# Linear attention into a gated MLP: one load on another queue, a longer row of opening matmuls, and another order of the first tile's second product

## The chip, the cores and the metric

The kernel runs on one core of one Trainium2 chip. A time is the time of one execution on the device, in microseconds (us). Eight runs of the kernel before gave a median of 286.97 us, from 286.65 to 289.56.

## The reference

Attention without a softmax feeds a two-layer MLP with a gate. `q`, `k` and `v` are 8 batches x 8 heads x 576 rows x 64, in float32.

```python
kv  = np.einsum('bhsd,bhse->bhde', k, v)
out = np.einsum('bhsd,bhde->bhse', q, kv)
rms = np.sqrt(np.mean(out * out, axis=-1, keepdims=True) + 1e-06)
x   = (out / rms * g_norm), its heads side by side: 4608 x 512
h   = x @ w_in                       # 512 x 2048
g   = h * (1.0 / (1.0 + np.exp(-1.702 * h)))
y   = g @ w_out                      # 2048 x 512
```

## The kernel before

**Tiles.** The 4608 rows are cut into nine row tiles of 512: one for the first 512 rows of each batch, `t` = 0 to 7, and a last one, `t` = 8, for the eight remainders of 64 rows. For each tile `dense` computes the hidden layer (`Hidden.mm`, L438: 16 column blocks of 128, four matmuls each; `gate` on ScalarE, L447) and then the product with `w_out` (`project`, L475: four row blocks `mo` of 128, sixteen matmuls `fo` each). While tile `t` is in `dense`, the attention of batch `t + 1` is woven into it. `units1` and `units2` hold that work: a unit filed under a number runs after the hidden block, or the step of the product, with that number. A step is one matmul of L475. So the numbers in `at2(...)` set where on TensorE a piece of attention stands, and also the order in which its instructions reach VectorE and ScalarE.

**Order.** The program runs with a schedule written out by hand: each engine takes its instructions in the order in which the Python code emits them, and semaphores do the rest.

**The opening.** Nothing can be woven into batch 0, so it runs by itself, head pair by head pair (four pairs): transpose `q` (L393), `kv` (L376), a copy to `kvb` (L383), `out` (L259), the sum of squares `ss` (L339), `ln` and `rs` on ScalarE (L341, L347), and `apply` on VectorE (L353), which writes the MLP's input `xT`. Before that TensorE runs 64 short matmuls on zeros (L572) and some long ones (`busy`, L562) whose results nobody reads.

**Queues.** SP's queue loads pair 0 of `k`, `q` and `v` of batch 0 in float32 (L147); VectorE and ScalarE cast them to half precision (L553 to L555). All else in the opening comes through GpSimd's queue, which casts as it loads: pairs 1 to 3 of batch 0 (`early_load`, L91), `w_in` (L166), `w_out` (L193), and `q`, `k`, `v` of batch 1 (L91, L112). Eight semaphores serve that queue in turn, so that the ninth load waits for the landing of the first, the tenth for that of the second, and so on. GpSimd also sets two constants, `ident` and `ones2` (L152 to L163), ahead of its first load.

**Batch 1 inside tile 0.** This is where the `at2` numbers of the diff belong. `pack_k` (L218) copies a pair of `k` into `kpad` on VectorE, `kv` (L227) multiplies it with `v`, `keep_kv` (L240) copies the result of two pairs to `kvb` on VectorE, `out` (L259) uses that, and `ss` and `apply` follow as above. PSUM has eight banks: three with the tag "att", three with "hT" and two with "o". In tile 0 the row blocks `mo` 0 and 1 of the second product hold two of the "hT" banks and `ss` has the third; the hidden blocks of tile 1 need all three again.

The steps of tile 0 are ordered by hand ("deep"), since `w_out` is still landing:

```python
steps = [(mo, 4 * i + k) for i in range(3) for mo in range(4) for k in range(4)]
steps += [(mo, f + k) for f in (12, 14) for mo in range(2) for k in range(2)]
steps += [(mo, 12 + k) for mo in (2, 3) for k in range(4)]
```

Of the kernel before, what the change touches and what calls it, by code (L numbers as in the profile page):

```python
# [12 lines left out]
P = 128  # L13
# [3 lines left out]
def kernel(  # L17
# [10 lines left out]
    nc = tc.nc  # L28
# [4 lines left out]
    NPAIR = H // 2  # L33
    FO = DFF // P
    KO = DM // P
# [8 lines left out]
    PE_ = 96  # L44
# [29 lines left out]
    vbuf = const.tile([P, NPAIR, 2 * NJ * D], F16)  # L74
# [5 lines left out]
    w_in_sb = const.tile([P, KO, DFF], F16)  # L80
# [6 lines left out]
    def early_src(n, b, c0, c1):  # L87
        return srcs[n][b, 2 * c0 : 2 * c1].rearrange("h (p j) d -> p h (j d)", j=NJ)

    def early_load(n, b, c0, c1):  # L90
        nc.gpsimd.dma_start(  # L91
            out=raw[n][0:PE_, c0:c1, :].rearrange("p c (l x) -> p (c l) x", l=2),
            in_=early_src(n, b, c0, c1),
        )
# [45 lines left out]


    first = {}
    for n in "kqv":
        first[n] = stage.tile([P, H, J * D], F32, name=f"{n}f", tag=f"{n}f")
        first[n] = first[n].rearrange("p h x -> p (h x)")[0:PE_, 0 : 2 * NJ * D]
        dst, src = first[n].rearrange("p (h x) -> p h x", h=2), early_src(n, 0, 0, 1)
        nc.sync.dma_start(out=dst, in_=src)  # L147
    g_row = const.tile([1, D], F32)
    nc.scalar.dma_start(out=g_row, in_=g_norm.unsqueeze(0))
    nc.vector.memset(ident, 0.0)  # L150
    nc.vector.memset(kvb[1], 0.0)
    nc.gpsimd.affine_select(  # L152
        out=ident,
        in_=ident,
# [6 lines left out]
    nc.gpsimd.memset(ones2, 0.0)  # L161
    nc.gpsimd.memset(ones2[0:D, 0:D], 1.0)
    nc.gpsimd.memset(ones2[D:P, D:P], 1.0)  # L163

    def load_w_in(f0, f1, k0=0, k1=KO):
        nc.gpsimd.dma_start(  # L166
            out=w_in_sb[:, k0:k1, f0 * P : f1 * P],
            in_=moe_w_in[k0 * P : k1 * P, f0 * P : f1 * P].rearrange(
                "(ko ki) f -> ki ko f", ki=P
            ),  # L170
        )

    for c in range(1, NPAIR):
        for n in "qkv":
            early_load(n, 0, c, c + 1)
            if c == NPAIR - 1 and n == "q":
                load_w_in(0, 4, 0, 1)
    load_w_in(0, 4, 1, 2)
    load_w_in(0, 4, 2, KO)
    load_w_in(4, GROUP)  # L180
    load_w_in(GROUP, 8)
# [267 lines left out]
    def dense(t, units1, units2, group, deep, hid=None):  # L449
        hid = hid or Hidden(t)  # L450
        gT = hid.gT
        if group and t:
            order = [(ko, fo) for part in ((0, 3, 1, 2), range(4, group)) for ko in (0, 1) for fo in part]
            order += [(ko, fo) for ko in range(2, KO) for fo in range(group)]
            for ko, fo in order:
                pool = (ps_h, "hT") if fo < 3 else (ps_a, "att") if fo == 3 else (ps_o, "o")
                hid.mm(ko, fo, *pool)
            for fo in range(group):
                hid.gate(fo)
        for fo in range(FO):  # L460
            if fo >= group:
                for ko in range(KO):
                    hid.mm(ko, fo)
                hid.gate(fo)
            for u in units1.get(fo, ()):
                u()

        osb = osbs[t] = opool.tile([P, 4, DM], F32, name="osb", tag="osb")
        os = {}

        def project(mo, fo):
            if fo == 0:
                pool, tag = (ps_h, "hT") if deep and mo < 2 else (ps_o, "o")
                os[mo] = pool.tile([P, DM], F32, name="o", tag=tag)
            nc.tensor.matmul(  # L475
                os[mo],
                gT[:, fo, mo * P : (mo + 1) * P],
                w_out_sb[:, fo, :],
                start=(fo == 0),
                stop=(fo == FO - 1),  # L480
            )
            if fo == FO - 1:
                by_act = mo % 2 if deep or t == B else 0 < t < B - 1 and mo < 2
                copy = nc.scalar.copy if by_act else nc.vector.tensor_copy
                copy(osb[:, mo, :], os[mo])  # L485
                if t == B:
                    store_rest(mo, 0, DM)
                elif t in HALVED and mo % 2:
                    store(t, mo - 1, mo + 1)

        def store_rest(mo, n0, n1):
            for g in range(2):
                rows = out[(2 * mo + g) * S : (2 * mo + g + 1) * S, n0:n1]
                if 2 * mo + g < EARLY:
                    p0 = SM % PE_
                    rows = rows[bass.DynSlice(NJ * p0 + SM // PE_, R, step=NJ), :]
                else:
                    rows = rows[SM:S, :]
                queue = (nc.sync, nc.scalar)[g]
                queue.dma_start(out=rows, in_=osb[g * R : (g + 1) * R, mo, n0:n1])  # L500


        def project_last(mo):
            for i, (n0, n1) in enumerate(LAST):
                o = ps_a.tile([P, n1 - n0], F32, name="oh", tag="att")
                for fo in range(FO):
                    nc.tensor.matmul(  # L507
                        o,
                        gT[:, fo, mo * P : (mo + 1) * P],
                        w_out_sb[:, fo, n0:n1],  # L510
                        start=(fo == 0),
                        stop=(fo == FO - 1),
                    )
                copy = nc.vector.tensor_copy if i else nc.scalar.copy
                copy(osb[:, mo, n0:n1], o)
                store_rest(mo, n0, n1)

        if deep:
            steps = [(mo, 4 * i + k) for i in range(3) for mo in range(4) for k in range(4)]
            steps += [(mo, f + k) for f in (12, 14) for mo in range(2) for k in range(2)]  # L520
            steps += [(mo, 12 + k) for mo in (2, 3) for k in range(4)]
        else:
            steps = [(mo, fo) for mo in range(4 - (t == B)) for fo in range(FO)]
        for n, (mo, fo) in enumerate(steps):
            project(mo, fo)
            for u in units2.get(n, ()):
                u()
        if t == B:
            project_last(3)
        if t < EARLY:  # L530

            n = 0
            while n < SM:
                mo, j, p = n // P, n // PE_, n % PE_
                m = min((mo + 1) * P, (j + 1) * PE_) - n
                nc.sync.dma_start(
                    out=out[t * S : (t + 1) * S, :][bass.DynSlice(NJ * p + j, m, step=NJ), :],
                    in_=osb[n % P : n % P + m, mo, :],
                )
                n += m  # L540
        elif t < B and t not in HALVED:
            store(t, 0, J)

    def store(t, j0, j1):
        nc.sync.dma_start(
            out=out[t * S : t * S + SM, :].rearrange("(p j) m -> p j m", j=J)[:, j0:j1],
            in_=osbs[t][:, j0:j1],
        )
# [3 lines left out]

    nc.scalar.copy(qraw[0:PE_, 0, :], first["q"])  # L553
    nc.vector.tensor_copy(kraw[0:PE_, 0, :], first["k"])
    nc.vector.tensor_copy(vbuf[0:PE_, 0, :], first["v"])  # L555


    idle_ps = ps_h.tile([P, SM], F32, name="idle", tag="hT")
# [1 line left out]
    def busy(n):  # L560
        for _ in range(n):
            nc.tensor.matmul(  # L562
                idle_ps,
                kvb[1][:, 0, :],
                kvb[1].rearrange("p c r -> p (c r)"),
                start=True,
                stop=True,
            )


    for _ in range(64):
        nc.tensor.matmul(  # L572
            idle_ps[:, 0:D], kvb[1][:, 0, :], kvb[1][:, 0, 0:D], start=True, stop=True
        )
    busy(4)
    a0.q(0)
    busy(2)
    a0.kv(0)
# [57 lines left out]
    nc.gpsimd.dma_start(out=g_all, in_=g_norm.unsqueeze(0).to_broadcast([P, D]))  # L636

    osbs = {}
    HALVED = (2, 3, 4, 5, 6)
    live = {0: a0}  # L640

    def start(b):
# [2 lines left out]
    for t in range(NT):  # L645
# [3 lines left out]
        def at1(i, f, *args):  # L649
            u1.setdefault(i, []).append(lambda: f(*args))  # L650

        def at2(i, f, *args):
            u2.setdefault(i, []).append(lambda: f(*args))

        def of(b, name, *args):
            return lambda: getattr(live[b], name)(*args)

        if t == 0:
# [8 lines left out]
            for c in range(NPAIR):  # L667
                at1(12, of(1, "pack_q", c))
                at2(9 + 3 * c, of(1, "q", c))
                at2((21, 21, 38, 38)[c], of(1, "pack_k", c))  # L670
                at2((36, 37, 46, 47)[c], of(1, "kv", c))
                o = (41, 43, 52, 53)[c]
                at2(o, of(1, "out", c))
                if c == NPAIR - 1:
                    at2(48, load_kv, 2)
                at2((45, 48, 56, 58)[c], of(1, "ss", c))
                at2((48, 51, 56, 60)[c], of(1, "apply", c))
        elif b < B:
            if t == 1:
                at2(46, setattr, live[1], "ss_pool", Attention.ss_pool)  # L680
# [3 lines left out]
            f0 = 5 if t == 1 else 2  # L684
# [48 lines left out]
```

## Time and profile before

| | us |
|---|---|
| median of 8 runs | 286.97 |
| the profiled execution's own time | 286.98 |
| its span, first to last instruction | 285.2 |
| TensorE busy | 278.9 |
| ScalarE busy | 155.9 |
| VectorE busy | 118.9 |
| GpSimd busy | 59.6 |

The span leaves out 1.8 us of the profiled execution that lie ahead of its first and behind its last instruction. PE stands for TensorE's matmuls, PEld for its weight loads, DVE for VectorE, ACT for ScalarE, POOL for GpSimd and SP for SyncE. In the timeline a row gives its start, its length, the engine, the line and the operation with "out<-in", and in brackets how long the engine sat idle before it and what ended that. A matmul's length runs to its modelled end, so that rows of matmuls overlap: how often they start tells the pace.

### The profile page before, as it was taken

To read this page: it belongs to the slowest core of one execution; us is meant where nothing else is said; L and a number is where in the kernel's file an instruction comes from. 1 tells how busy PE (TensorE), PEld (TensorE's weight loads), DVE (VectorE), ACT (ScalarE), POOL (GpSimd) and SP (SyncE) were. 2 spreads that over 40 slices of the span, in tenths; PEclk is the share of its full clock that TensorE was granted. 3 is DMA by queue.
4 is the path that set the end of the run, shared out by engine and by line. 5 is a ranking of instruction groups with operands and counts; after the bars stand their busy time and mean duration, and the time that the engine had idled before them with its cause. 6 is when DMAs were issued, how large, how long until landed. Compare 5 with 4: busy or idle time off the path is not lost.

```text
span 285.2 us, 4458 instructions
## 1 busy us (share of the span) xinstructions
PE 278.9 (98%) x1768; PEld 137.2 (48%) x1768; DVE 118.9 (42%) x230; ACT 155.9 (55%) x273; POOL 59.6 (21%) x86
## 2 busy tenths in 40 slices
PE   8899999999999999999999999999999999999995
PEld 6434554455445544554455445544454444444443
DVE  1650557527661657147713852286327400110001
ACT  2678439766575645574468536763666365016400
POOL 8762372111211121112011401130002100000000
PEclk9999999999999999999999999999999999999999
DMA  8999999996589456953797278915401410011022
GB/s 174 194 199 205 205 236 248 254 258 115 125 165 249 69 137 166 244 89 67 223 206 143 40 213 224 163 37 184 85 0 37 121 65 0 2 70 77 0 76 74
DMA packets 55158, 38.78 MB, mean 136 GB/s; under 512 B 31282, under 2 KB 52018, under 8 KB 55010
## 3 DMA queue, kind: packets, MB, share of 16 engines
q0 software_dynamic: 16048, 15.59, 33.6%
q1 hardware_dynamic: 38688, 22.39, 29.8%
q10 hardware_dynamic: 402, 0.52, 0.6%
q8 instruction: 14, 0.23, 0.3%
q14 instruction: 6, 0.05, 0.1%
HBM read 36.73 MB, written 9.44 MB: 162 GB/s over the span
## 4 chain that ended last, share of the span: by engine, by line
PE 93%; DMA 4%; ACT 1%; POOL 0%; issue 0%; DVE 0%
PE hT L438 43%; PE o L475 42%; PE kvp L227 3%; DMA vbuf<-in_v_dram 2%; DMA qraw<-in_q_dram 2%; PE outR L291 2%; PE oh L507 1%; PE ss L339 1%; PE q L416 0%; ACT sq L279 0%; PE outT L270 0%; PE outT L259 0%; ACT ln L341 0%; POOL kraw L91 0%; ACT rs L347 0%
## 5 line engine op out<-in xcount | busy, mean ns | idle before, releaser
L475 PE MATMUL o<-w_out_sb,gT 128*128 128x512 f16 x560 | 130.7, 379 | 0.0
L447 ACT ACTIVATE gT<-hT 128x512 f16<-128x512 f32 x144 | 84.5, 601 | 75.9 <-PE hT L438 75.8
L438 PE MATMUL hT<-xT,w_in_sb 128*128 128x512 f16 x512 | 116.5, 379 | 0.1
L438 PEld LDWEIGHTS <-w_in_sb 128*128 128x128 f16 x576 | 54.5, 98 | 62.5 <-issue 0.6
L475 PEld LDWEIGHTS <-gT 128*128 128x128 f16 x560 | 53.0, 98 | 56.7 <-issue 0.4
L485 DVE COPY osb<-o 128x512 f32<-128x512 f32 x20 | 13.8, 691 | 62.4 <-PE o L475 62.4
L323 POOL TENSOR_TENSOR x<-xr,g_all 128x512 f16<-128x512 f32 x12 | 15.2, 1271 | 70.3 <-DVE xr L316 46.3
L218 DVE COPY kpad<-kraw 64x576 f16<-64x576 f16 x56 | 25.0, 446 | 1.3
L240 DVE CAST kvb<-kvp 64x128 f16<-64x128 f32 x28 | 8.1, 289 | 39.9 <-PE kvp L227 39.7
L302 DVE TENSOR_REDUCE sum<-sq 128x8 f32<-128x512 f16 x24 | 15.8, 679 | 19.1 <-ACT sq L299 19.1
L112 POOL DMA_DIRECT2D kraw<-in_k_dram x16 | 10.0, 627 | 50.9 <-DVE kpad L218 35.0
L316 DVE TENSOR_TENSOR xr<-outR,sum 128x512 f32<-128x512 f32 x24 | 15.5, 686 | 11.1 <-ACT sum L313 11.1
L112 POOL DMA_DIRECT2D vbuf<-in_v_dram x16 | 9.7, 610 | 31.6 <-PE kvp L227 28.1
L323 DVE TENSOR_TENSOR x<-xr,g_all 128x512 f16<-128x512 f32 x12 | 15.2, 1267 | 0.7
L279 ACT ACTIVATE sq<-outT 128x512 f16<-128x512 f32 (+1 forms) x16 | 7.7, 486 | 13.5 <-PE outT L259 12.1
L299 ACT ACTIVATE sq<-outR 128x512 f16<-128x512 f32 x24 | 13.6, 590 | 2.0 <-PE outR L291 1.6
L227 PEld LDWEIGHTS <-kpad 128*128 128x128 f16 x252 | 11.1, 98 | 6.4
L438 PE MATMUL hT<-x_rem,w_in_sb 128*128 128x512 f16 x64 | 14.0, 379 | 0.0
L485 ACT COPY osb<-o 128x512 f32<-128x512 f32 x15 | 8.7, 582 | 6.3 <-PE o L475 6.3
L227 PE MATMUL kvp<-vbuf,kpad 128*128 128x64 f16 x252 | 11.9, 193 | 0.0
L312 ACT ACTIVATE sum<-sum,eps_t 128x16 f32<-128x16 f32 x12 | 3.7, 308 | 15.0 <-DVE sum L302 14.9
L341 ACT ACTIVATE ln<-ss,eps_t 128x512 f32<-128x512 f32 (+1 forms) x16 | 9.4, 586 | 2.3 <-PE ss L339 2.2
(64 smaller groups left out, 144.7 us busy)
## 6 DMA issues: line engine op xcount, KB each, us to landing
qf<-in_q_dram SPq DMA_DIRECT2D x5, 1024.0 KB, 9.3
out_dram<-osb SPq DMA_DIRECT2D x10, 512.0 KB, 2.9
kraw<-in_k_dram POOLq DMA_DIRECT2D x12, 288.0 KB, 7.1
vbuf<-in_v_dram POOLq DMA_DIRECT2D x12, 288.0 KB, 5.4
out_dram<-osb SPq DMA_DIRECT2D x6, 192.0 KB, 5.7
w_in_sb<-in_moe_w_in_dram POOLq DMA_DIRECT2D x4, 256.0 KB, 7.5
w_out_sb<-in_moe_w_out_dram POOLq DMA_DIRECT2D x2, 512.0 KB, 13.8
w_out_sb<-in_moe_w_out_dram POOLq DMA_DIRECT2D x4, 256.0 KB, 10.2
```

The lines of the kernel that those rows point to most:

```text
L112: nc.gpsimd.dma_start(out=raw[n][l * PH : (l + 1) * PH, c0:c1, 0 : NH * D], in_=srcs[n][b].rearrange("(c l) (p j) d -> l p c (j d)", l=2, ...
L218: nc.vector.tensor_copy(out=kpad[r, c, :, l * D : (l + 1) * D], in_=kraw[r, c, 0 : NH * D].rearrange("p (j d) -> p j d", j=NH),)
L227: nc.tensor.matmul(self.kvp[:, c, :], kpad[:, c, j, :], vbuf[:, c, j * D : (j + 1) * D], start=(j == 0), stop=(j == NH - 1),)
L299: nc.scalar.activation(sq, t, AFT.Square)
L302: nc.vector.tensor_reduce(out=self.sum2[:, j % 2, :], in_=sq.rearrange("p (h d) -> p h d", h=H), op=ALU.add, axis=mybir.AxisListType.X,)
L316: nc.vector.tensor_mul(xr[:, i], self.o[j + i].rearrange("p (h d) -> p h d", h=H), s2[:, i, :].unsqueeze(2).to_broadcast([P, H, D]),)
L323: (nc.vector if i else nc.gpsimd).tensor_mul(self.x16[:, j + i, :].rearrange("p (h d) -> p h d", h=H), xr[:, i], g_all.unsqueeze(1).to_bro ...
L341: nc.scalar.activation(ln[:, 0:n], t[:, 0:n], AFT.Ln, bias=eps_t, scale=1.0 / D)
L438: nc.tensor.matmul(self.h[fo], w_in_sb[:, ko, fo * P : (fo + 1) * P], self.x[:, ko], start=(ko == 0), stop=(ko == KO - 1),)
L447: nc.scalar.activation(self.gT[:, fo, :], self.h[fo], AFT.Gelu_apprx_sigmoid)
L475: nc.tensor.matmul(os[mo], gT[:, fo, mo * P : (mo + 1) * P], w_out_sb[:, fo, :], start=(fo == 0), stop=(fo == FO - 1),)
L485: copy(osb[:, mo, :], os[mo])
```

## The change

It has six parts.

1. Pair 0 of `v` no longer comes through SP's queue with a cast on VectorE. It is the first load of GpSimd's casting queue and lands in `vbuf` directly.
2. GpSimd's constants `ident` and `ones2` are set behind its fifth load instead of ahead of its first. The order of the loads behind `v` of pair 0 is as before.
3. TensorE opens with 88 short matmuls instead of 64, and the four long ones behind them are gone.
4. In tile 0 the last steps of the second product are reordered: blocks 12 and 13 of `w_out` for all four `mo`, then blocks 14 and 15 for all four.
5. In the weaving of batch 1 into tile 0 some step numbers move by one to three.
6. The output of tile 7 is stored in two halves, as is that of tiles 2 to 6.

```diff
     first = {}
-    for n in "kqv":
+    early_load("v", 0, 0, 1)
+    for n in "kq":
...
     nc.vector.memset(ident, 0.0)
     nc.vector.memset(kvb[1], 0.0)
...
+    for n in "qkv":
+        early_load(n, 0, 1, 2)
+    early_load("q", 0, 2, 3)
     nc.gpsimd.affine_select(
...
     nc.gpsimd.memset(ones2[D:P, D:P], 1.0)
...
-    for c in range(1, NPAIR):
-        for n in "qkv":
+    for c in range(2, NPAIR):
+        for n in "qkv"[c == 2 :]:
             early_load(n, 0, c, c + 1)
...
             steps = [(mo, 4 * i + k) for i in range(3) for mo in range(4) for k in range(4)]
-            steps += [(mo, f + k) for f in (12, 14) for mo in range(2) for k in range(2)]
-            steps += [(mo, 12 + k) for mo in (2, 3) for k in range(4)]
+            steps += [(mo, f + k) for f in (12, 14) for mo in range(4) for k in range(2)]
...
     nc.vector.tensor_copy(kraw[0:PE_, 0, :], first["k"])
-    nc.vector.tensor_copy(vbuf[0:PE_, 0, :], first["v"])
...
-    for _ in range(64):
+    for _ in range(88):
         nc.tensor.matmul(
             idle_ps[:, 0:D], kvb[1][:, 0, :], kvb[1][:, 0, 0:D], start=True, stop=True
         )
-    busy(4)
     a0.q(0)
...
-    HALVED = (2, 3, 4, 5, 6)
+    HALVED = (2, 3, 4, 5, 6, 7)
...
                 at2((21, 21, 38, 38)[c], of(1, "pack_k", c))
-                at2((36, 37, 46, 47)[c], of(1, "kv", c))
-                o = (41, 43, 52, 53)[c]
+                at2((38, 39, 46, 47)[c], of(1, "kv", c))
+                o = (42, 44, 52, 53)[c]
                 at2(o, of(1, "out", c))
...
-                at2((45, 48, 56, 58)[c], of(1, "ss", c))
-                at2((48, 51, 56, 60)[c], of(1, "apply", c))
+                at2((45, 48, 56, 60)[c], of(1, "ss", c))
+                at2((48, 51, 56, 61)[c], of(1, "apply", c))
```

Within one step the units run in the order of the pairs `c`. At step 38 that is now: `kv` of pair 0, then `pack_k` of pairs 2 and 3. Before, `keep_kv` of pairs 0 and 1 came with step 37, ahead of those two `pack_k`; now it comes with step 39, behind them.

More of the change, by code (lines that the diff above doesn't have):

```diff
@@ L151, with load_w_in @@
     nc.vector.memset(kvb[1], 0.0)
+    def load_w_in(f0, f1, k0=0, k1=KO):
+        nc.gpsimd.dma_start(
+            out=w_in_sb[:, k0:k1, f0 * P : f1 * P],
+            in_=moe_w_in[k0 * P : k1 * P, f0 * P : f1 * P].rearrange(
+                "(ko ki) f -> ki ko f", ki=P
+            ),
+        )
+    for n in "qkv":
+        early_load(n, 0, 1, 2)
+    early_load("q", 0, 2, 3)
     nc.gpsimd.affine_select(
@@ L163 @@
     nc.gpsimd.memset(ones2[D:P, D:P], 1.0)
[L165 to L171, printed above, removed]
-    for c in range(1, NPAIR):
-        for n in "qkv":
+    for c in range(2, NPAIR):
+        for n in "qkv"[c == 2 :]:
             early_load(n, 0, c, c + 1)
```

## The prediction

> **What bounds the kernel now.** I read the page first:
>
> ```profile
> PE 278.9 (98%) x1768; PEld 137.2 (48%) x1768; DVE 118.9 (42%) x230; ACT 155.9 (55%) x273; POOL 59.6 (21%) x86
> ```
>
> TensorE is busy nearly all the time, so a gain or a loss is a hole in its row that closes or opens. Next the chain that ended last, cut to the first 17 us:
>
> ```profile
> 1.79 5.54 DMA qraw<-in_q_dram
> 7.33 0.28 issue
> 7.61 0.65 POOL kraw L91
> 8.27 6.22 DMA vbuf<-in_v_dram
> ...
> 14.53 0.40 PE kv L376 x12
> ```
>
> The opening hangs on GpSimd's casting queue, not on TensorE: TensorE stands still from 13.95 until the last pair of v lands. The weight loads show one more wait of that kind, and it is the last one on the loads:
>
> ```profile
> 17.82 0.76 PEld L438 LDWEIGHTS <-w_in_sb 128*128 128x128 f16 x5 [0.48 <-DMA w_in_sb<-in_moe_w_in_dram]
> ```
>
> From there to the end the matmuls of the timeline start at an even pace, with one hole of 0.24 us at 45.86, where an `ss` waits for ScalarE's copy of an output bank:
>
> ```profile
> 45.22 0.59 ACT L485 COPY osb<-o 128x512 f32<-128x512 f32 x1
> 45.86 0.38 PE L339 MATMUL ss<-sq,ones 128*128 128x512 f16 x1
> ```
>
> So what the change can win is how much sooner the casting queue delivers, plus that 0.24. What it can lose is any wait that it puts into the woven stretch from 38 to 48 us. The rows of VectorE there:
>
> ```profile
> 35.00 1.87 DVE L218 COPY kpad<-kraw 64x576 f16<-64x576 f16 x4
> 39.25 0.59 DVE L240 CAST kvb<-kvp 64x128 f16<-64x128 f32 x2 [2.38 <-PE kvp L227]
> 39.87 1.88 DVE L218 COPY kpad<-kraw 64x576 f16<-64x576 f16 x4
> 42.58 0.59 DVE L240 CAST kvb<-kvp 64x128 f16<-64x128 f32 x2 [0.83 <-PE kvp L227]
> ```
>
> and the k loads behind the second four copies (the tile view, cut to 30.2 to 33 us), issued at 30.28 and 32.72, which land at 38.5 and 39.26:
>
> ```profile
> L112 POOL DMA_DIRECT2D kraw<-in_k_dram x2: 592/592/592, 30.3 to 32.7; - x2
> ...
> DMA to landing us min/median/max: 6.5/7.4/8.2
> ```
>
> **What the Trainium skill says.** "DMA: Bandwidth & Descriptors", § Issuing engines are not separate DMA queues: loads of all queues run on the same 16 DMA engines, so v on another queue brings no bandwidth of its own. The DMA view agrees: both queues together moved 0.22 MB between 5 and 6 us. Same page, § Queues, rings and completion order: descriptors of one ring are taken in order; here the casting loads land in the order of their issue. "TensorE: Matmul & The Clock Gate", § Architectural detail: VectorE and ScalarE take instructions strictly in order; the rows above agree. Same page, Part 1: TensorE runs at half clock until a window of about 3.4 us was busy. Here the short matmuls start every 53 ns from 1.28, the long ones every 427 ns, and full pace (216 ns) is seen from about 6.7.
>
> **Parts 1 to 3, the opening.** TensorE's side: 24 more short matmuls cost 24 x 0.053 = 1.28; four long ones, 4.68 to 6.51, go (1.83). It is free at 5.97 instead of 6.51, and q is cast at 5.21 + 0.83 = 6.04. Twelve transposes (0.47, up to 0.15 more at half clock) and two long ones (0.44) later, kv(0) could start at about 7.1 instead of 7.78. The v cast on VectorE (0.56) is gone. TensorE gains 0.6, but the casting queue decides.
>
> The queue: its first issue moves from 1.79 to about 0.75, where SP issues too. DMA view in slices: 2 to 4 us, SP's loads alone move 0.27 MB/us; casting moves 0.01 MB from 4 to 5, 0.12 from 5 to 6, 0.19 from 6 to 7, then about 0.195 each us, without a break to 41. Carried back at full rate it begins at 7 - 0.32/0.195 = 5.36. SP's three float32 loads (0.29 MB each) hold the engines until then: 0.88/0.27 from 1.8 gives 5.1. With two, SP is done at 1.8 + 0.59/0.27 = 4.0, and the first cast, 1.04 earlier than now, is ready by then; I take 4.2, 1.15 earlier. Ahead of the old loads now stands v of pair 0: 96 x 768 half-precision values, 0.147 MB, 0.75 us at 0.195. Net, all later casts land **0.4 us earlier** (0.15 to 0.6). v of pair 0 lands at 4.2 + 0.75 + 1.2 (lag of the first load now) = 6.2, ahead of 7.1.
>
> The constants cost POOL 1.02 to 1.79, about 0.8, now at about 4.1 to 5.0: `ident` is needed at 6.1, `ones2` at 7.6, so both are in time. Behind them stand k and v of pair 2, q of pair 3 and w_in: k issues at about 5 and its data are due when five loads have moved, 4.2 + 5 x 0.75 = 8.0. From issue to first byte took 2.35 for the first load. 5.0 + 2.35 = 7.4: no hole in my count, up to 0.4 if GpSimd needs longer to restart. The semaphore wait moves on by one load: w_in waits for v of pair 0 (6.2, POOL free at 6.9), k3 for q1, v3 for k1, all landed before POOL gets there. TensorE follows the queue (kv(3), then the w_in wait at 17.82), so it gains the same 0.4.
>
> **Parts 4 and 5, the woven stretch**, on the clock of before, since loads and TensorE shift alike. At step 38 the second `pack_k` four now stand before `keep_kv`. VectorE does the first at 38.5, must then wait for the second landing: 39.29, then 39.77 and 40.24 (0.475 apart), then `keep_kv` at 40.72 and 41.02, ended at 41.31. `out(0)` reads that, 0.07 later: **41.38**. TensorE arrives there at 39.91 + one matmul 0.22 = 40.13. **Stall 1.25.** Behind `out(0)` in TensorE's queue stands all of tile 0's rest; nothing overtakes.
>
> Then, counted from `out(0)` (T), with matmul 0.216, kv 0.262, ScalarE's 0.42 from a matmul's start, and its row spacing (sq 0.48, ln 0.71, rs 0.54): out(1) T+0.65, ss(0) 1.08, ss(1) 2.47, out(2) 3.54, out(3) 3.97, ss(2) 4.84. sq of pairs 2 and 3 run at 4.13 and 4.61, ln(2) 5.25 to 5.96, rs(2) 6.00. ss(3) has ss(2)'s bank and waits for ln(2): 6.01 instead of 5.91 (0.10). ScalarE's copy of mo 1 now stands behind rs(2): 6.54 to 7.12; tile 1's first hidden block takes that bank: 7.17 instead of 6.87 (0.30). ln(3) ends at 7.70 and holds back the next block (0.14), VectorE's copy of mo 0, behind apply(2), another (0.09). Sum 0.63 instead of the 0.24 that go: **+0.39**. w_out[14:16] is needed four matmuls later (0.86), but nothing waited for it: nought; without that cover its landing (43.29) would bind. TensorE's work is the same.
>
> **Part 6.** One more issue on SP at about 248; the whole store now goes at 254.83 and lands in 3.9, while the chain ends at 281.78. Nought; uncovered it would cost its landing.
>
> **Sum:** -0.4 + 1.25 + 0.39 = +1.24 on the profiled 286.98, itself the median of 286.97: **288.2**.
>
> **Rivals.**
> - *Slower by more (30%).* POOL's constants open a hole behind the fifth load. Against it: 7.4 < 8.0; for it: the one latency that I know is of a first load. From 0.2 us on it tells: 0.4 eats the gain, 286.98 + 1.64 = 288.6, and 288.8 with another 0.2 in the woven stretch.
> - *No stall at `out(0)` (16%).* If the second k load lands over 1 us sooner against TensorE than before, because TensorE loses at half clock what the queue wins, the 1.25 vanishes: 286.98 - 0.4 + 0.39 = 287.0. For it: only the landing, not VectorE's work, is in the way. Against: both shift together at 17.82.
> - *Faster (4%).* The casts go 1.04 or more earlier with v's bytes free, and no stall: 286.98 - 1.1 - 0.24 = 285.6 at best; it takes a queue with spare bandwidth, and 4 to 41 us show none.
> - *Nothing happens.* v could be no earlier than before; it lands at 6.2 against 7.17 + 0.56, so the change does what it says, but the path is elsewhere. It gives the likeliest without the 0.4, inside its range.
>
> **How the numbers follow.** The likeliest has 50% and by itself reaches from 287.8 to 288.7 (gain 0.15 to 0.6, stalls 0.2 either way). Within 0.5%, about what a measurement of this kernel can tell from no change, is 285.5 to 288.4: three quarters of the likeliest, a fifth of the slower rival, the third: 0.60. Slower 0.38, faster 0.02. The range 286.8 to 288.9 leaves out the fast case and the worst of the slow one.
>
> **What would show it.** Casting's first bytes near 3.1 and full rate by 4.3; v3 landing near 14.1; kv(0) near 7.2, kv(3) near 14.1, 17.82 near 17.4. Four `pack_k` in a row, broken by a wait for kraw, ahead of `keep_kv`; an `out` L262 that waits over 1 us for `kvb`. An `ss` that waits for `ln`, and hidden blocks of tile 1 held by `osb` and `ln`. Wrong if `keep_kv` is done before 40, or if casts land more than 0.8 earlier.

## The result, and the profile after

The changed kernel takes 290.30 us (median of 11 runs, 289.27 to 290.84) against 286.94 for the kernel before (32 runs): a ratio of 1.0106, 95% interval 1.0088 to 1.0123. The forecast was 288.2 and its range ended at 288.9. The profiled execution took 289.83, its span 288.1 (285.2 before), so the profile shows 2.9 us of the loss. The busy times on its page:

```profile
PE 278.3 (97%) x1788; PEld 137.2 (48%) x1788; DVE 118.4 (41%) x229; ACT 156.0 (54%) x273; POOL 60.4 (21%) x87
```

TensorE's work is the same, so again the loss is holes. To place them I compare when the same matmul starts in both traces. At the 41st hidden matmul (24.0 us before) the changed kernel is 0.77 late, at the 81st, behind the woven stretch (50.6 before), 2.52, and behind a hole at 169.5 it is 2.88. So the opening lost 0.77 (predicted: 0.4 gained), the woven stretch lost 1.75 (predicted 1.64), and 0.35 come from a place that the prediction did not name.

**Opening.** TensorE in the timeline of the changed kernel:

```profile
10.83 0.38 PE L379 MATMUL kv<-vbuf,kraw 96*64 96x64 f16 x12 [0.53 <-DMA vbuf<-in_v_dram]
...
13.92 0.39 PE L441 MATMUL hT<-xT,w_in_sb 128*128 128x512 f16 x1 [1.56 <-DMA w_in_sb<-in_moe_w_in_dram]
...
15.31 0.38 PE L379 MATMUL kv<-vbuf,kraw 96*64 96x64 f16 x12
```

The weight loads of the same kernel, the one row that waits at the end of the opening:

```profile
18.59 0.33 PEld L441 LDWEIGHTS <-w_in_sb 128*128 128x128 f16 x3 [0.47 <-DMA w_in_sb<-in_moe_w_in_dram]
```

`kv` of pair 3 starts at 15.31 (14.53 before), and the wait that stood at 17.82 now stands at 18.59. Up to 12 us the change did what was hoped: q of pair 3 lands at 11.43 instead of 11.76. The next load, the first of `w_in`, lands at 13.87 instead of 12.35. The stage view shows why: busy time per engine, then TensorE's clock, the DMA engines' mean load and what they moved. First the kernel before:

```profile
core 0: us, PE busy (x) PEld busy (x) DVE busy (x) ACT busy (x) POOL busy (x), PEclk, DMA share, GB/s
4.00:6.00 2.00, 2.00 (x21) 1.12 (x18) 0.58 (x1) 0.79 (x1) 2.00 (x4) 1.00 1.13 221
6.00:8.00 2.00, 1.80 (x28) 0.84 (x26) 0.83 (x2) 0.05 (x1) 1.31 (x3) 1.00 1.28 195
...
10.00:12.00 2.00, 1.85 (x28) 0.89 (x27) 0.97 (x4) 1.78 (x4) 1.94 (x3) 1.00 1.22 189
12.00:14.00 2.00, 1.86 (x18) 0.79 (x17) 1.52 (x3) 2.00 (x4) 1.52 (x3) 1.00 1.27 198
```

and the changed kernel:

```profile
10.00:12.00 2.00, 1.40 (x30) 0.74 (x28) 1.22 (x3) 1.63 (x4) 2.00 (x4) 1.00 1.06 111
12.00:14.00 2.00, 0.44 (x13) 0.31 (x14) 1.36 (x3) 1.26 (x3) 0.96 (x2) 1.00 1.18 166
```

111 GB/s instead of 189, while the DMA engines count as nearly as busy (1.06 against 1.22; over 1 where packets overlap): packets are not missing, they take longer. A packet of the casting queue normally takes 0.06 to 0.10 us. Below I call those over 0.2 us *long*, and sum their time up to 16 us: 2.9 us in the kernel before, 19.1 in the changed one, single packets up to 1.0.

**Woven stretch.** VectorE in the timeline of the changed kernel:

```profile
35.77 1.87 DVE L221 COPY kpad<-kraw 64x576 f16<-64x576 f16 x4
39.44 0.45 DVE L221 COPY kpad<-kraw 64x576 f16<-64x576 f16 x1 [1.80 <-DMA kraw<-in_k_dram]
40.19 1.41 DVE L221 COPY kpad<-kraw 64x576 f16<-64x576 f16 x3 [0.31 <-DMA kraw<-in_k_dram]
41.63 0.59 DVE L243 CAST kvb<-kvp 64x128 f16<-64x128 f32 x2
```

and TensorE, where it waits for the last of these:

```profile
42.28 0.39 PE L262 MATMUL outT<-qT,kvb 128*128 128x512 f16 x1 [1.22 <-DVE kvb L243]
```

As predicted: `keep_kv` behind four copies that wait twice for `kraw`, and `out(0)` 1.38 late by the pace of the matmuls before it (1.25 predicted). Behind it four small holes of 0.08, 0.28, 0.16 and 0.10 (0.61; 0.63 predicted), and the hole of 0.24 is gone.

**The third place.** TensorE in the timeline of the changed kernel, at the first hidden matmul of a later tile:

```profile
169.52 0.81 PE L441 MATMUL hT<-xT,w_in_sb 128*128 128x512 f16 x3 [0.19 <-DMA xT<-x]
```

### The profile page after: what moved, and what is told of

Same layout as the page of the kernel before. It is cut to its first block, busy times and chain, and to the rows that moved or that the text cites. A ratio compares the mean times of both kernels' runs of the same rounds, so it can differ in the third digit from the quotient of the medians.

```text
span 288.1 us, 4497 instructions
## 1 busy us (share of the span) xinstructions
PE 278.3 (97%) x1788; PEld 137.2 (48%) x1788; DVE 118.4 (41%) x229; ACT 156.0 (54%) x273; POOL 60.4 (21%) x87
## 4 chain that ended last, share of the span: by engine, by line
PE 82%; DMA 11%; POOL 3%; DVE 2%; issue 1%; ACT 1%; POOLq 0%; SPq 0%
PE hT L441 39%; PE o L478 36%; DMA w_out_sb<-in_moe_w_out_dram 6%; PE kvp L230 2%; DMA kraw<-in_k_dram 2%; DMA vbuf<-in_v_dram 2%; PE outR L294 2%; PE oh L510 1%; DMA xT<-x 1%; POOL qraw L91 1%; POOL vbuf L91 1%; POOL kraw L91 1%; PE ss L342 1%; PE outT L262 0%; DVE kpad L221 0%
## 5 line engine op out<-in xcount | busy, mean ns | idle before, releaser
L305 DVE TENSOR_REDUCE sum<-sq 128x8 f32<-128x512 f16 x24 | 15.8, 679 | 19.1 <-ACT sq L302 19.1
```

The costliest lines, as they stand in the source:

```text
L305: nc.vector.tensor_reduce(out=self.sum2[:, j % 2, :], in_=sq.rearrange("p (h d) -> p h d", h=H), op=ALU.add, axis=mybir.AxisListType.X,)
```

## The experiments

Times are medians; ratios are against the kernel before on the same chip, with 95% intervals. "Late by" compares one profile with that of before at the 41st and 81st hidden matmul and at the end.

| kernel | us | ratio | late by, 24 / 51 us / end | long packets to 16 us | v of pair 3 lands |
|---|---|---|---|---|---|
| before | 286.9 to 287.1 | 1 | | 2.9 | 14.49 |
| after | 290.30 | 1.0106 [1.0088, 1.0123] | 0.77 / 2.52 / 2.85 | 19.1 | 15.27 |
| e1 | 289.71 | 1.0087 [1.0064, 1.0111] | 2.82 / 2.82 / 3.21 | 27.6 | 15.43 |
| e2 | 288.80 | 1.0069 [1.0045, 1.0092] | 0.08 / 2.01 / 1.96 | 10.8 | 14.66 |
| e3 | 289.00 | 1.0069 [1.0046, 1.0092] | 0.78 / 0.77 / 1.01 | 17.9 | 15.25 |
| e4 | 287.78 | 1.0026 [1.0002, 1.0050] | 0.41 / 0.41 / 0.38 | 11.6 | 14.96 |
| f1 | 290.70 | 1.0110 [1.0072, 1.0149] | 1.93 / 2.50 / 4.02 | 23.2 | 15.15 |
| f2 | 289.65 | 1.0085 [1.0056, 1.0115] | 0.70 / 1.60 / 3.34 | 19.9 | 14.53 |
| f3 | 289.38 | 1.0087 [1.0053, 1.0121] | 0.85 / 0.90 / 1.25 | 15.7 | 14.59 |
| f4 | 287.46 | 1.0009 [0.9993, 1.0025] | -0.15 / -0.15 / -0.18 | 1.3 | 14.26 |
| g1 | 287.56 | 1.0016 [1.0004, 1.0028] | 0.16 / 0.84 / 0.80 | 11.0 | 14.07 |
| g2 | 288.38 | 1.0046 [1.0034, 1.0059] | 0.03 / 0.80 / 1.12 | 17.2 | 14.56 |
| g3 | 287.58 | 1.0019 [1.0005, 1.0033] | -0.30 / 0.28 / 0.24 | 4.8 | 14.21 |
| h1 | 288.52 | 1.0056 [1.0032, 1.0080] | 1.20 / 1.20 / 1.16 | 6.2 | 14.78 |
| h2 | 287.77 | 1.0023 [1.0003, 1.0043] | 0.10 / 0.10 / 0.42 | 16.6 | 13.99 |
| i1 | 286.98 | 1.0000 [0.9987, 1.0014] | -0.43 / -0.55 / -0.02 | 3.6 | 14.09 |

### Two halves: e1 and e2

e1 has the opening (parts 1 to 3) alone, e2 the steps and the weave (parts 4 and 5) alone.

> The kernel before with parts 1 to 3 of the change alone (v of pair 0 first in the casting queue, constants behind the fifth load, 88 short matmuls); the weave, the steps and the stores of before. Theory A (the opening of the changed kernel lost 0.78 us because of these parts): the first w_in matmul and kv(3) stand about 0.8 later than before, no stall at out(0), the time is before + 0.8, about 287.7. Rival B (the slow stretch of the casting queue between 10 and 13 us was chance): the opening gains 0.4 as predicted, about 286.6.

> The kernel before with parts 4 and 5 of the change alone (order of the last w_out blocks, step numbers of batch 1 in tile 0). Theory: the second pack_k four wait for kraw ahead of keep_kv, out(0) waits 1.25 to 1.4, the ss, osb and ln waits behind it add 0.6 and 0.24 go: before + 1.7, about 288.6. Rival: the k load, which starts earlier against TensorE than in the changed kernel, has landed by then, and the stall is under 0.5: about 287.4.

e2 came out as expected (+1.7; its `out(0)` waits 1.56, since TensorE is there sooner). e1 lost 2.65, over three times what theory A said: the opening is at fault, and it is worse than the one profile of the changed kernel shows. The stage view of e1:

```profile
core 0: us, PE busy (x) PEld busy (x) DVE busy (x) ACT busy (x) POOL busy (x), PEclk, DMA share, GB/s
...
9.50:13.00 3.50, 2.02 (x35) 1.06 (x37) 1.41 (x3) 2.72 (x5) 2.65 (x4) 1.00 1.08 129
13.00:16.50 3.50, 2.89 (x29) 1.05 (x25) 1.12 (x2) 1.96 (x4) 2.96 (x4) 0.51 1.24 191
16.50:20.00 3.50, 3.08 (x17) 1.14 (x12) 0.95 (x2) 1.09 (x2) 2.15 (x3) 0.51 1.44 196
```

Again a slow stretch (129 GB/s), and behind it TensorE's granted clock is at half for 6.83 us (13.07 to 19.90). A second question, taken up under f2.

### The woven stretch: g3 and f1

```diff
-                at2((21, 21, 38, 38)[c], of(1, "pack_k", c))
+                at2((21, 21, 40, 40)[c], of(1, "pack_k", c))
```

g3 is e2 with this edit, f1 the whole changed kernel with it.

> Parts 4 and 5 as in e2, but the second two pack_k under step 40, behind keep_kv; opening of the kernel before. Theory: the wait at out(0), 1.56 in e2, falls to under 0.3 and the holes behind it (0.6) stay: before + 0.4, about 287.4. Rival (the wait only moves, to kv of pairs 2 and 3 or to their keep_kv): 288 or more.

> The changed kernel whole, but the second two pack_k filed under step 40 instead of 38, so that they stand behind keep_kv on VectorE. Theory (two pack_k that wait for kraw hold keep_kv back): the wait of 1.38 us at out(0) goes, the holes behind it of 0.6 stay, so 1.4 less than the changed kernel, about 288.9. Rival (out(0) would wait for something else, the landing itself or kv): less than 0.5 of it goes, 289.8 or more. It is also a second look at the opening of the changed kernel: theory B (chance) has v3 landing at 14.5 or earlier, theory A at 15.2 to 15.4.

In g3 VectorE's order is the one wanted (timeline of g3):

```profile
35.65 0.92 DVE L218 COPY kpad<-kraw 64x576 f16<-64x576 f16 x2
39.38 0.59 DVE L240 CAST kvb<-kvp 64x128 f16<-64x128 f32 x2 [2.81 <-PE kvp L227]
40.00 1.40 DVE L218 COPY kpad<-kraw 64x576 f16<-64x576 f16 x3
```

The hole at `out(0)` falls from 1.56 to 0.20, the four behind it stay (0.61), and the stretch costs 0.58 against 1.93 in e2. Both predicted terms are confirmed separately. In f1 the hole falls too (1.38 to 0.20) and the stretch costs 0.57, but the time does not: this execution lost 1.93 in the opening, with the clock at half for 6.83 us, and 1.5 more at 66.5, where `outR` waits for the transpose of q (`qTd`), issued at 55.6 and landed 10.8 later (8.1 in the changed kernel). f1's expectation on the time missed; why that transfer is later in f1 and f2 is open.

### Which part of the opening: e3, e4, f3, f4

e3 is e1 with the constants first; f3 is the move of v alone; e4 the constants alone; f4 the matmuls alone.

```diff
 f3, and e3 with 88 short matmuls and no busy(4):
+    early_load("v", 0, 0, 1)
-    for n in "kqv":
+    for n in "kq":
...
-    nc.vector.tensor_copy(vbuf[0:PE_, 0, :], first["v"])
 e4: the four constants behind q of pair 2, nothing else
 f4:
-    for _ in range(64):
+    for _ in range(88):
...
-    busy(4)
```

> Parts 1 and 3 alone: v of pair 0 first in the casting queue and 88 short matmuls, but GpSimd's constants ahead of its first load as before. Theory A1 (the slow stretch comes from the constants behind the fifth load, which make the sixth load late): no slow stretch, 0 to 0.4 gained or lost by the start of the queue alone, 286.6 to 287.0. Theory A2 (it comes from v in the casting queue, one more load ahead of w_in, whatever the constants do): the first w_in matmul 0.8 or more later than before, about 287.7 to 288.2.

> Part 2 alone: GpSimd's constants behind q of pair 2, its fourth load; v of pair 0 stays on SP's queue, 64 short matmuls and the four long ones stay. Theory A1 (constants cause the slow stretch): casts between 10 and 13 us at 0.09 to 0.14 MB per us, about 0.8 lost, 287.7. Theory A2 (v's move causes it): the queue as before or up to 0.4 earlier, 286.6 to 287.0.

> Part 1 alone: v of pair 0 first in the casting queue; constants first, 64 short matmuls and four long ones as before. Theory A2 (v's move costs): as e3, 288.5 to 289.0. Rival E (the four long matmuls that part 3 takes away cost, not v): 286.6 to 287.2, within 0.2 of before.

> Part 3 alone: 88 short matmuls and no long ones; v of pair 0 and the constants as before. Theory A2 (v's move costs): within 0.2 of before, 286.8 to 287.2, q(0) earlier and kv(0) as before. Rival E (part 3 costs, through TensorE's clock): 288 or more, with a mean granted clock of 0.994 or less in most runs.

The move of v is what costs most: f3 alone +2.4, e3 +1.9, both more than either theory had said. The matmuls alone cannot be told from nothing (rival E falls), the constants alone cost 0.7, as A1 had it. So the rival on which the prediction spent its 30%, a hole made by the constants, is real but the smaller part.

### Why moving v costs: g1, g2, h1, h2

I gave each casting load its packets by order and size and took the time from issue to first packet. In e3 and f3 the first four loads have 2.0 to 3.2 us between them, in the kernel before 3.4 and more from the second on. Theory L: packets that come up soon behind their issue are the slow ones.

g1 delays only the issue of the first `w_in` load; g2 gives the moved v its lead back (`ident` first, `ones2` on VectorE); h1 moves v but lets SP go on loading it as its third load into a tile that nobody reads; h2 takes SP's third load away and adds nothing (pair 0 of batch 0 is computed from k in place of v).

```diff
 g1:
+                for _ in range(5):
+                    nc.gpsimd.memset(lag, 0.0)
                 load_w_in(0, 4, 0, 1)
 h2:
-    for n in "kqv":
+    for n in "kq":
...
-    nc.vector.tensor_copy(vbuf[0:PE_, 0, :], first["v"])
+    nc.vector.tensor_copy(vbuf[0:PE_, 0, :], first["k"])
```

> The kernel before with five memsets of a spare tile on GpSimd directly ahead of the first w_in load; nothing reads it. It should issue that load about 1.2 later (7.5 instead of 6.36), while the load behind it (k of pair 3) waits to 7.6 anyway. Theory L (packets of a casting load that come up for their turn less than about 3.7 us behind the load's issue take up to 1 us each instead of 0.08): the packets of the w_in load that take over 0.2 us sum to 4 us or more (0.5 before), the queue runs below 0.15 MB per us for 1 us or more between 10 and 13, v of pair 3 lands at 14.9 or later (14.49), time 287.4 to 288.5. Rival F (this is chance, or it goes with v in the queue only): long packets of 1 us or less, time within 0.2 of before.

> Parts 1 and 3 (v of pair 0 first in the casting queue, 88 short matmuls), and GpSimd's constants out of its way: ident first as before, while its queue is not ready anyway, and ones2 set by VectorE. The loads are issued from 1.3 on without a break, w_in at about 6.4 as in the kernel before. Theory L: no slow stretch at w_in, v of pair 3 lands at 14.1 or earlier, time 286.6 to 287.2, the gain that was predicted. Theory A2 (v in the casting queue costs, whatever the lead): 288.5 to 289.5 as in e1, e3 and f3, with a mean granted clock of 0.994 or less in most runs.

> As f3 (v of pair 0 first in the casting queue, all else as before), but SP still loads v in float32 as its third load, into a tile that nobody reads. So the casting queue starts no earlier than before and carries one load more. Theory L (the third SP load gives the casting queue its distance between issue and transfer): packets over 0.2 us in the first five casting loads sum to 3 us or less (13.1 in f3), full rate from 5.4, every later cast 0.75 later than in the kernel before, v of pair 3 at 15.2. Theory A2 (a casting load of v ahead of the others slows them): 8 us or more in the first five loads, v of pair 3 at 15.7 or later.

> The kernel before without SP's load of v of pair 0; VectorE casts k in its place, so that pair 0 of the first batch is computed from k instead of v. It measures by itself the term by which the prediction had the casting queue start earlier (1.15). As predicted: full rate from 4.2, v of pair 3 at 13.4 (14.49 before). Theory L: the queue starts at 4.2 but its first packets come less than 3.3 us behind their issue; packets over 0.2 us in the first five loads sum to 6 us or more (2.1 before), and v of pair 3 lands at 13.8 to 14.3, so that half or more of the 1.15 is lost.

h1 and h2 decide what slows the queue. The stages of h2 (columns as above):

```profile
4.00:6.00 2.00, 1.37 (x21) 0.64 (x18) 1.23 (x2) 0.67 (x1) 2.00 (x4) 1.00 1.16 162
6.00:8.00 2.00, 1.79 (x32) 1.03 (x33) 0.81 (x3) 0.16 (x1) 2.00 (x4) 1.00 1.16 148
```

and of h1:

```profile
4.00:6.00 2.00, 2.00 (x21) 1.12 (x18) 0.68 (x1) 0.72 (x1) 2.00 (x4) 1.00 1.14 227
6.00:8.00 2.00, 2.00 (x33) 1.00 (x32) 0.67 (x3) 0.11 (x1) 1.78 (x4) 1.00 1.31 197
```

With v ahead in the casting queue but SP's third load kept (h1), the queue runs as before (197 GB/s), and its first five loads have 0.7 us of long packets (13.1 in f3). Without SP's third load and without v (h2), the same queue runs at 162 and 148 and has 11.8. So v in the queue does not slow it; the queue is slow where SP's third load is missing and it starts 1 us sooner, close behind its issues. h2 starts sooner, as predicted (first packet at 3.9), and lands v of pair 3 at 13.99 instead of 13.4: 0.5 of the 1.15 arrive. Although it loads less, it is not faster (+0.23%): in its profile TensorE now waits for v of pair 2, which lands at 11.66 instead of 10.94 (timeline of h2):

```profile
11.79 0.38 PE L376 MATMUL kv<-vbuf,kraw 96*64 96x64 f16 x12 [1.43 <-DMA vbuf<-in_v_dram]
```

In time, however, the added load is the larger part. By their medians h1, with the queue at full rate, is 1.6 us slower than the kernel before, h2 0.9, and f3, which has both changes, 2.4; the intervals of h1 and h2 overlap. h1's 288.52 is where theory A2 had put a moved v, 288.5 and more, although its packets are those of theory L. What one more load does in h1 is to make TensorE wait where it did not before (timeline of h1):

```profile
11.26 0.38 PE L380 MATMUL kv<-vbuf,kraw 96*64 96x64 f16 x12 [0.69 <-DMA vbuf<-in_v_dram]
...
12.88 0.60 PE L397 MATMUL q<-ident,qraw 96*64 96x96 f16 x12 [0.46 <-DMA qraw<-in_q_dram]
```

In 16 of its 20 executions TensorE's clock then fell, which is taken up under f2.

g1 shows the same at one load: issued at 8.12 instead of 6.36 (later than the 7.5 intended), first packet 1.99 behind instead of 4.03, 5.4 us of long packets instead of 0.5, 123 GB/s between 11 and 12. But v of pair 3 did not land later in that execution, a miss, and the cost is small (+0.16%). g2 missed on both sides: `w_in` has its distance back (3.93), the opening loses nothing, but v of pair 0 and q, k and v of pair 1 still come 2.0 to 3.3 behind their issues (10.7 us of long packets), and 288.4 is 1.3 better than e1, not the hoped gain.

Over the 168 casting loads up to v of pair 3 in all 16 profiles: under 3.0 us between issue and first packet, 2.50 us of long packets a load (45 loads); 3.0 to 3.5, 0.89; 3.5 to 4.0, 0.73; from 4.0 on, 0.25 (34 loads). No long packet is found from 20 to 40 us, where loads land 6.5 to 17 us behind their issues.

The kernel before shows the same by itself, late and far from the change. Its k loads issued at 82.89, 112.71 and 142.53 find the queue empty; their first packets come 1.4 us behind the issue, and 11.3, 13.0 and 11.0 us of their packets' time are long. The loads issued directly behind them wait their turn for 4.3 to 4.6 us and have 0, 0 and 0.9. Over the 256 casting loads issued after 70 us in the 16 profiles it is 11.2 us a load below 1.6 us (108 loads) and 0.6 from 3.0 on (123 loads).

In the opening the relation scatters: the changed kernel's k, v and q of pairs 2 and 3 came 2.3 to 2.6 behind and had under 1 us each, while e2, which opens like the kernel before, had 9.0 in its first `w_in` load at 3.65. So one load in one profile proves little, and what a packet waits for is not in the trace.

### TensorE's clock: f2

```diff
+    busy(2)     # ahead of kv(1), and again ahead of kv(2)
...
+    busy(4)     # ahead of the first w_in matmul
```

> Parts 1 to 3 as in e1, with eight more long matmuls on zeros: two ahead of kv(1), two ahead of kv(2), four ahead of the first w_in matmul (8 x 0.216 = 1.73 us of TensorE, in places where e1 stands still for 0 + 1.10 + 0.85). Theory C (most of what the opening loses is TensorE's clock, which falls to half for 6.83 us because TensorE stands still too long between 9.7 and 13.1): the mean granted clock is 0.998 or more in nearly all runs and the time falls from 289.7 to about before + 0.8, 287.9. Theory D (the loss is the casting queue's alone): 289.7 or more, as e1.

The half of theory C that is about the clock holds: it stays (0.998 or more in all six executions; 0.994 or less in five of six of e1, in seven of twelve of the changed kernel, in 22 of 147 of the kernel before), and in its profile f2 leaves the opening 0.70 late instead of e1's 2.82. The time does not fall: 289.65 is what theory D said. Four transfers now come too late for TensorE, where e1 shows no wait: `v` at 39.4 (a hole of 0.42), `w_out` at 45.2 (0.64), the transposed `q` at 64.6 (0.55) and `xT` at 80.2 (0.88).

So what a fall costs is not settled. In the kernel before, executions in which the clock fell have a median of 288.4, the others 286.95; in h1 it is 289.1 and 287.5. In the changed kernel it is 290.3 and 290.0 only. A late load can bring both the fall and the longer time, and no run here separates the two.

When it falls can be read from the 16 profiles. I cut time into stretches of 3.41 us from where the clock first becomes full, and add up the own time at full clock of the matmuls that start in each. The clock falls in e1, f1, f3 and h1, behind stretches filled to 0.477, 0.500, 0.500 and 0.492; up to 20 us it falls behind no other stretch at full clock, and the emptiest of those are filled to 0.516 (the changed kernel and e2) and 0.547 (h2). Where the line runs depends on how one counts: most transposes and `kv` matmuls start in pairs at the same moment, and with each pair counted once and matmuls cut at the ends of a stretch, the four are filled to 0.34 to 0.37 and all others to 0.43 or more. Either way the clock falls behind the emptiest stretches; a threshold is not shown. "TensorE: Matmul & The Clock Gate", § What's actually happening, has a free-running window of 3413 ns, with which the 3.41 and 6.83 us agree, and the fall behind an idle window; here a window that matmuls filled to a third was enough.

### A try for a better kernel: i1

> A try for a kernel better than both: the kernel before, with ones2 set by VectorE instead of GpSimd, so that every casting load is issued about 0.4 earlier while SP's three loads still hold back its transfer; and ss of pair 3 one step later (59, apply at 61), where a matmul of the second product fits into the hole of 0.24 at 45.86. Theory L: packets over 0.2 us up to 13 us sum to 3 us or less, the w_in load is issued at 6.0 and its packets start 4 us or more behind it; 0.2 to 0.4 less than the kernel before, 286.6. Rival (the queue is bound by bytes alone and the hole of 0.24 comes back elsewhere): within 0.1 of before.

The edit worked (`w_in` issued at 6.00, first packet 4.37 behind, no long one in it; 0.55 ahead at 51 us) and the time did not move: TensorE then waits for the next batch's v, where it had come just in time before. TensorE in the timeline of i1:

```profile
57.52 0.42 PE L227 MATMUL kvp<-vbuf,kpad 128*128 128x64 f16 x9 [0.38 <-DMA vbuf<-in_v_dram]
```

No version here beats the kernel before.

### The hole at 169.5

It is in all eight kernels with two SP loads in the opening (0.07 to 0.37 us), h2 among them, and in none of the eight with three, h1 among them. So it goes with SP's number of loads, not with v. The second transpose of `x` on SP's queue is issued 4.81 us behind the first (3.96 before), though `x` is ready at the same distance (4.40) in both. The traces show where it stands: in all 16 profiles SP pauses for 0.45 to 0.47 us between the end of its 79th instruction and the start of its 80th, where most follow within 0.03 to 0.06. With three loads the 80th is the first of these two transposes, with two loads it is the second, the one that TensorE waits for. Why SP pauses there is not shown.

## Why the prediction was wrong, point by point

- *Opening, TensorE's side.* Right: `kv(0)` at 7.06 (7.2 predicted), v of pair 0 at 5.83 (6.2). GpSimd's first issue was at 1.30, not 0.75 (it stood idle for 0.84 first); that did no harm, as the queue was at full rate from 4.2 all the same.
- ***The step that failed: "Net, all later casts land 0.4 us earlier".*** In the changed kernel it holds up to q of pair 3 (0.33), then the queue lost 1.1 up to v of pair 3. The sum was 1.15 for the earlier start less 0.75 for v's bytes, both at 0.195 MB/us. It took SP's third load for a hindrance only. h2 measured the first term alone: 0.5, not 1.15, since its queue, which starts close behind its issues, runs at 148 to 162 GB/s; and the kernel got 0.9 slower by it. In the changed kernel, the constants included, it came to +0.77 instead of -0.4. In all eight kernels with v moved, v of pair 3 lands at 14.53 to 15.43, in none ahead of the 14.49 of before. With it failed "so it gains the same 0.4", that TensorE moves as the queue does: in f3 v of pair 3 is only 0.10 late, TensorE 0.85.
- *Constants.* "7.4 < 8.0: no hole" was right for k of pair 2 (first packet at 7.99), and looked at the wrong load: the delay stays in the distance of every load behind, and it was `w_in` (2.56 behind) that had 9.4 us of long packets. The price that the rival put on it, 0.4, was too small: e4 lost 0.7.
- *TensorE's clock.* Missing from the sum. The new opening gets TensorE to its waits sooner and makes them longer, and in more than half of the executions the clock fell. In the profiled execution it did not fall. That explains little of the 0.5 by which the median (290.30) lies above it: the five executions without a fall have a median of 290.04, and the slowest of all (290.84) is one of them.
- *Woven stretch.* Right in mechanism and size: 1.38 for 1.25, 0.61 for 0.63, hole of 0.24 gone; g3 confirms both terms.
- *Not foreseen:* 0.35 at 169.5, where with one load fewer SP's pause comes ahead of the other transpose.
- *Part 6.* Nought: from 170 us to the end the distance between the two traces changes by 0.03.
- e1 and e2 together lose 4.4, the changed kernel 3.4. That a late opening hides part of the wait for `kraw`, which does not depend on TensorE, would explain it; this is argued, not shown.

## What to carry to other kernels

A load that holds back a queue may also be what lets it run at full rate: before counting an earlier start as a gain, look at how far its packets run behind their issues, and at which load a delay of the issuing engine is paid. Gains in an opening that waits for data are worth little where the next load comes just in time, and waits that leave most of 3.4 us empty can also bring TensorE's clock down. File copies that wait for a transfer behind those that don't.

## What the runs showed of the hardware

- Casting packets close behind their issue: up to 1.3 us (f2, f3) instead of 0.08, with the averages by distance above. A casting load on an empty queue (first packet 1.4 behind) has 11 us of such packets.
- TensorE's clock fell behind the four emptiest of the stretches of 3.41 us (matmuls in 0.34 to 0.37 of the time) and not behind 0.43 and more.
- SP paused for 0.45 to 0.47 us ahead of its 80th instruction in all 16 profiles.
- Fetches of 16 KB on a queue of kind "instruction", 0.95 to 0.98 us each, seen at 7.19 in the changed kernel, 8.73 in f4 and 11.60 before. In each of the three one of the next three landings came 1.5 to 1.8 us behind the one ahead of it, where 0.6 to 0.75 is usual: q of pair 2 at 9.40, k of pair 2 at 10.89, k of pair 3 at 13.93. So it is, with 1.05 to 2.2 us, in 15 of the 16 profiles. That one causes the other is not shown.
